# Turning the pooled keys of four batches on VectorE and moving them by DMA, in an attention and hidden-layer kernel

## The chip, the cores and the metric

The kernel runs on one core of a Trainium2 chip. The core has five engines with a queue of instructions each: TensorE (PE in the profile, with its weight loads as PEld) multiplies matrices and writes PSUM; VectorE (DVE), ScalarE (ACT) and GpSimd (POOL) work on elements; SyncE (SP) does no arithmetic here and issues DMAs. A DMA is carried out by 16 DMA engines that all queues share. Each engine takes its instructions in the order of the program and waits on semaphores for the others. SBUF is the memory of 128 partitions that the engines work in; PSUM, eight banks of 2 KB per partition, takes what TensorE writes.

The metric is the device time of one execution in microseconds. Less is better.

## The reference

The first half is attention over pooled keys and values, for 8 batches of 8 heads, 576 positions and 64 numbers per head, all f32:

```python
k_p = k.reshape(B, H, Sp, pool, D).mean(axis=3)      # Sp = 72 pooled keys, of 8 positions each
v_p = v.reshape(B, H, Sp, pool, D).mean(axis=3)
scores = scale * np.matmul(q, k_p.transpose(0, 1, 3, 2))
scores = scores - np.max(scores, axis=-1, keepdims=True)
attn = np.exp(scores)
attn = attn / (np.sum(attn, axis=-1, keepdims=True) + 1e-09)
x = np.matmul(attn, v_p)        # then (batch, position) become 4608 rows, the heads 512 columns
```

The second half takes these 4608 rows x 512 columns through two matrix products with a sine between them:

```python
h = x @ w_in                    # 512 -> 2048
s = np.sin(alpha * h)
g = h + s * s / (alpha + 1e-09)
out = g @ w_out                 # 2048 -> 512
```

## The kernel before, in words

**Stages.** After a head start (batch 0, some 20 us), the kernel runs nine units of about 55 us each, from 0 to 8. A unit computes the hidden values h and g of 512 rows of x (`hidden`, line 816), which it stores to DRAM; beside it runs the attention of a later batch. After the units, up to the end, the second product is computed (`outputs`, its matmuls at L1328). Both products use Strassen's scheme on 2 x 2 blocks, so that sums and differences of blocks are formed by VectorE and GpSimd, and TensorE does 7 block products in place of 8.

**Slots.** A unit has 28 slots: four groups J of 256 + 256 hidden columns, and seven block products (k = 0 to 6) in each. A slot's product is four matmuls of 256 columns (L844). `carry(u)` (line 1169) is a list written by hand: `at(slot, f)` puts a step into a slot, and in that slot its instructions are given to all engines, in between those of the products. So the order on each engine is fixed when the program is built, and no scheduler changes it.

**What a unit u of 1 to 6 carries.** It computes the attention of batch b = u + 1, whose rows are needed by the next unit. In the order of slots: the scores (`two_scores`, slots 3 and 5, matmuls at L317); the row maxima and differences on VectorE (`shifts`, L340 and L341); in slot 6 the load of the batch's values (`load_v`, L140 and L145); in slot 7 the load of the queries of batch u + 2 (`load_q`, L84 and L105); from slot 8 the exponentials on ScalarE, the normalization on GpSimd (L374), and the turn of the attention weights on VectorE in 32 x 32 blocks (`turn`, L501 to L511); in slot 14 sixteen DMAs which put the turned blocks into their places (`move`, L521, tile `aM`); in slots 23 and 24 the turn of the next queries (`turn_q`, L228 and L233), and their sixteen DMAs (L243); in slot 25 the products with the values (`all_values`, L610 and L623). The hidden values of each group J are stored by two DMAs (`store_g`, L1060) from one of two buffers `h`.

**The keys.** `load_k` (line 116) loads the keys of four heads by one DMA (L121) into a buffer `kvin`, of which there are two and which the values use too; two loads make a batch. GpSimd adds up the 8 positions of a pooled key in three additions per half (`pool_rows`, L131), and the sums come to the tile `kp`: 96 partitions, partition 24 hp + x for the head pair hp and the group x of three keys, and on each partition three keys j of two heads of 64 numbers. There is one buffer for `kp`. `k_t` (line 273) then turns them: three transposes on TensorE (L278), one for each j, into a bank of PSUM, from which one copy on VectorE (L279) brings them to `kblk`, with the three j woven together, so that the 72 keys of a head stand in a row. `kblk` has two buffers, for even and odd batches. The score matmuls have 64 queries as the stationary operand, read `kblk` as the moving one and write 72 columns of PSUM.

Before the change, unit u loads and adds up the keys of batch b + 1 in slot 12, and turns them in slot 26 of the same unit. They are read in slot 3 of the next.

**SyncE's queue.** Nearly all DMAs are issued by SyncE, in the order of the slots. The program gives them eight semaphores in turn, and lets each DMA wait for the one eight places before it.

Of the kernel before, what the change touches and what calls it, by code (L numbers as in the profile page):

```python
# [13 lines left out]
F32 = mybir.dt.float32  # L14
# [26 lines left out]
class Kernel:  # L41
# [216 lines left out]
    def attention(self, b):  # L258

        nc, D, H, Sp, NP, S = self.nc, self.D, self.H, self.Sp, self.NP, self.S  # L260
        kb, ex = self.kblk[b % 2], self.ex
# [11 lines left out]
        def k_t():  # L273
# [4 lines left out]
                nc.tensor.transpose(ps[:, j, :], kp[:, j].rearrange("p e d -> p (e d)"), self.ident[:NP * m, :NP * m])  # L278
            nc.vector.tensor_copy(out=kb[:].rearrange("p hp (x j) -> p j hp x", j=3), in_=ps.rearrange("p j (hp x) -> p j hp x", hp=NP))  # L279

        def q_t(i, copy=nc.scalar.copy):

            n = rows[i]
            x = self.qm[b][:n].rearrange("p (t hp x) -> p t hp x", t=5, hp=NP)[:, i]
            if b not in self.qt:
                self.qt[b] = self.qt_view(self.q_tile(0))
            ps = self.abank([P, NP, P])
            for hp in range(NP):
                nc.tensor.transpose(ps[:, hp, :n], x[:, hp], self.ident[:n, :n])  # L289
            copy(out=self.qt_tiles(b)[:, i, :, :n], in_=ps[:, :, :n])  # L290

        def columns(hp, i):

            if b < 2:
                if i == 4:
                    return [(0, self.qt_tiles(b)[:, 4, hp, 0:64])]
                return [(c, self.qt_tiles(b)[:, i, hp, c:c + 64]) for c in range(0, rows[i], 64)]
            if i < 4:
                at = self.q_at(i) + P * hp
                return [(64 * c, self.qt[b][:, at + 64 * c:at + 64 * c + 64]) for c in range(2)]  # L300
            return [(0, self.qt[b][:, 512 + 64 * hp:576 + 64 * hp])]

        def two_scores(j):

            x = (self.turn + 1) % 5
            tiles = []
            for i, banks in ((2 * j, (x, 7)), (2 * j + 1, (5, 6))):
                m = 6 if i == 3 else NP
                ps = [self.psum([P, m, Sp], c) for c in banks]
                tiles.append((i, m, ps))  # L310
                for t in (i, 4) if i == 3 else (i,):
                    for hp in range(NP):
                        r0, h = (64 * (hp // 2), NP + hp % 2) if t == 4 else (0, hp)
                        for r, q in columns(hp, t):
                            for e in range(2):
                                s = slice(64 * e, 64 * e + 64)
                                nc.tensor.matmul(ps[e][r0 + r:r0 + r + q.shape[-1], h, :], q[s], kb[s, hp, :], start=True, stop=True)  # L317
            for i, m, ps in tiles:
                self.shifts.append(lambda i=i, m=m, ps=ps: shifts(i, m, ps))
            two_shifts()  # L320
            if j == 0:
                two_shifts()

        def two_shifts():

            self.shifts.pop(0)()

        def shifts(i, m, ps):

            y = E(i).rearrange("p (e h) k -> p e h k", e=2)  # L330
            if i % 2:
                ps, y = [self.PS[:, 5:7, 0:m * Sp].rearrange("p e (h k) -> p e h k", h=m)], [y]
            else:
                y = y[:, 0], y[:, 1]
            for z, o in zip(ps, y):
                w = list(z.shape)[:-1]
                mx = self.sm.tile([P, 12], F32, name="mx2")[:, 0:m * (1 + i % 2)]
                if i % 2:
                    mx = mx.rearrange("p (e h) -> p e h", e=2)
                nc.vector.tensor_reduce(out=mx, in_=z, axis=AX, op=OP.max)  # L340
                nc.vector.tensor_tensor(out=o, in0=z, in1=mx.unsqueeze(len(w)).to_broadcast(w + [Sp]), op=OP.subtract)  # L341
# [258 lines left out]
        def all_values():  # L600
# [26 lines left out]
            for hp in hps:  # L627
                to_x(ps[hp].rearrange("p (t j) -> p j t", t=4), hp, 0, 512)
            to_x(rest, slice(0, 4), 512, 64)

        return SimpleNamespace(**{f.__name__: f for f in (k_t, q_t, products, score, two_scores, two_shifts, exp, norm, new_a, turn, move, values, values_rest, all_values,
                                                          k_head, k_last, q_head, rest_q, products_head, soft_shift, soft_exp, norm_head, norm_rest, a_head, a_rest)})


# [534 lines left out]
    def carry(self, u):  # L1169

        nc = self.nc
        x = defaultdict(list)
        at = lambda slot, f, *a: x[slot].append(lambda: f(*a))
        last = self.B - 1
        b = u + 1
        if u == 0:
            A0, A = self.att[:2]
            at(1, A0.rest_q)
            at(1, A0.a_head, 1, (5, 6, 2))
            at(1, self.refine)  # L1180
            at(2, A0.values, (2, 3), (2, 1), 1, 1)
            at(2, A0.score, 4)
            at(2, self.sums_of_x, 0, 2)
            at(2, self.sums_of_x, 0, 3)
            at(2, self.load_w_in_part, 2)
            at(2, self.load_w_in_part, 3)
            at(2, self.pairs_q, 1, (0, 1))
            at(3, self.pairs_q, 1, (2, 3, 4))
            at(4, self.combine_w_in, 1, (0, 1, 2, 3), self.nc.gpsimd)
            at(4, A.q_t, 0, self.nc.vector.tensor_copy)  # L1190
            at(4, A.q_t, 1, self.nc.vector.tensor_copy)
            at(4, A.k_t)
            at(7, self.load_v, 1)
            at(7, lambda: self.pool_v())
            for i in range(2):
                at((6, 11)[i], A.two_scores, i)
            at(13, A.two_shifts)
            for i in range(2, 5):
                at((8, 8, 9)[i - 2], A.q_t, i)
            at(9, A0.exp, 4)  # L1200
            for i in range(4):
                at((9, 9, 15, 15)[i], A.exp, i)
                at((10, 10, 16, 16)[i], A.norm, i)
                at((13, 13, 19, 19)[i], A.turn, i)
            at(8, self.combine_w_in, 2, (0, 1, 2, 3), self.nc.gpsimd)
            at(13, A0.norm_rest)
            at(17, self.combine_w_in, 3, (0, 1), self.nc.gpsimd)
            at(17, self.combine_w_in, 3, (2, 3), self.nc.gpsimd)
            at(22, A0.a_rest)
            at(24, lambda: A0.values_rest((5, 6, 7, (self.turn + 1) % 5)))  # L1210
            for r in (32, 96):
                at(3, self.nc.gpsimd.memset, self.aM[r:r + 32, :, 704:736], 0.0)
            at(19, A.move, range(3))
            at(20, A.move, (3,), nc.scalar, (0,))
            at(21, A.move, (3,), nc.scalar, (1,))
            at(26, A.all_values)
            at(9, self.load_q, 2)
            at(23, self.inner_w_in)
            for e in range(2):
                at(12, self.load_k, 2, e)  # L1220
                at(17, lambda e=e: self.pool_k[e]())
            at(27, self.att[2].k_t)
            turn = 23
        else:
            at(0, self.sums_of_x, u, 2)
            at(0, self.sums_of_x, u, 3)
        if 0 < u < last:
            A = self.att[b]
            for i in range(2):
                at((3, 5)[i], A.two_scores, i)  # L1230
            at(6, A.two_shifts)
            for i in range(4):
                at((8, 9, 10, 10)[i], A.exp, i)
                at((9, 10, 11, 12)[i], A.norm, i)
                at((12, 13, 13, 13)[i], A.turn, i)
            at(14, A.move, range(4))
            at(6, self.load_v, b)
            at(12, lambda: self.pool_v())
            for i in range(2):
                if b < last:  # L1240
                    at(12, self.load_k, b + 1, i)
                    at(12, lambda i=i: self.pool_k[i]())
            at(25, A.all_values)
            if b < last:
                at(26, self.att[b + 1].k_t)
            if 2 < u + 2 <= last:
                at(7, self.load_q, u + 2)
            at(2, self.inner_x, u)
            turn = 22
        elif u:  # L1250
            turn = None
        if turn and u + 2 <= last:
            for part in range(4):
                at(((turn, turn + 1) if u == 0 else (23, 24))[part] if part < 2 else turn + part, self.turn_q, u + 2, part)
        if u + 1 < self.NU:
            at(27, self.sums_of_x, u + 1, 0)
            at(27, self.sums_of_x, u + 1, 1)
        return x
# [336 lines left out]
```

## Time and profile before

| | us |
|---|---|
| median of three runs | 904.47 (903.34 to 905.92) |
| the profiled execution | 904.95 |
| its span, from the first to the last instruction | 903.2 |
| TensorE busy in it | 895.0 |
| VectorE, ScalarE, GpSimd busy | 681.0, 449.1, 212.6 |
| matmuls of the first product (L844), busy | 440.9 |
| score matmuls with `kblk` (L317), busy | 19.9 |
| transposes of the keys (L278), busy | 2.9 |
| the copies behind them (L279), busy | 3.9 |

A line of the chain of waits or of a timeline begins with a start and a length in us, then names the engine, the line of the program, what is done to which tiles, and how many instructions are merged; in square brackets stands how long the engine was idle before, and what ended that. An f32 matmul shows as two records (two passes), and a few records are missing from the trace. A transpose on TensorE shows as one. The granted clock of TensorE is 1.00 throughout. The units' products lie between 20 and 516 us of the span, and the scores of units 3 to 6 begin at 202.5, 257.8, 312.8 and 367.9.

### The profile page before, as it was taken

The numbers are of one execution on the slowest core, as the hardware profiler recorded it, in microseconds if no ns is written. First come the engines' busy times: TensorE is split into PE (matmuls) and PEld (weight loads), VectorE is DVE, ScalarE is ACT, GpSimd is POOL, SyncE is SP. The second block draws the span as 40 slices with busy tenths as digits, with TensorE's granted clock in tenths as the row PEclk, the third lists the DMA queues.
The fourth block names the chain that finished last, engine by engine and source line by source line (L and its number), as shares of the span: only waits on it lengthen the run. The fifth ranks groups of instructions, "written<-read, shape, count | busy, mean of one in ns | idle before, by whom it ended". The sixth has DMA issues, their size and how long they took to land.

```text
span 903.2 us, 17920 instructions
## 1 busy us (share of the span) xinstructions
PE 895.0 (99%) x7002; PEld 815.1 (90%) x7002; DVE 681.0 (75%) x1012; ACT 449.1 (50%) x1072; POOL 212.6 (24%) x216
## 2 busy tenths in 40 slices
PE   8999999999999999999999999999999999999998
PEld 5787888888888888888888999999999999999998
DVE  7685766768577685764557799979798888889895
ACT  5686776877768778687976611111111111111111
POOL 5688552824438253430000000000000000000000
PEclk9999999999999999999999999999999999999999
DMA  9965867759577595648217246261618162533401
GB/s 253 255 200 151 219 166 196 194 149 270 145 212 186 174 238 138 180 141 298 93 67 232 98 139 205 53 198 40 224 27 227 37 192 72 171 92 123 141 14 40
DMA packets 128746, 141.12 MB, mean 156 GB/s; under 512 B 46920, under 2 KB 95704, under 8 KB 128664
## 3 DMA queue, kind: packets, MB, share of 16 engines
q1 hardware_dynamic: 125880, 137.88, 53.5%
q10 hardware_dynamic: 2784, 2.11, 0.9%
q8 instruction: 55, 0.90, 0.4%
q14 instruction: 27, 0.22, 0.1%
HBM read 75.37 MB, written 47.19 MB: 136 GB/s over the span
## 4 chain that ended last, share of the span: by engine, by line
PE 95%; DVE 2%; ACT 2%; DMA 1%; POOL 0%; SPq 0%; ACTq 0%; issue 0%; DVEq 0%
PE PS L844 44%; PE PS L1328 41%; PE PS L1024 3%; PE PS L317 2%; PE PS L610 2%; PE PS L623 1%; DMA home<-in_k_dram 1%; DVE x L1283 1%; ACT s L1001 0%; DVE s L1283 0%; DVE r L1283 0%; ACT s L994 0%; PE PS L568 0%; PE PS L289 0%; PE PS L278 0%; PE PS L566 0%
## 5 line engine op out<-in xcount | busy, mean ns | idle before, releaser
L844 PE MATMUL PS<-home,a 128*128 128x256 f32 x1104 | 258.0, 381 | 0.4 <-DVE h L819 0.2
L844 PEld LDWEIGHTS PS<-home,a 128*128 128x128 f32 x1104 | 205.2, 190 | 33.3 <-issue 5.0
L844 PE MATMUL PS<-home,as 128*128 128x256 f32 x768 | 182.9, 382 | 0.5 <-ACT PS L820 0.5
L844 PEld LDWEIGHTS PS<-home,as 128*128 128x128 f32 x768 | 141.6, 190 | 20.6 <-ACT PS L820 1.2
L1378 POOL TENSOR_TENSOR cc<-cc,cb 128x576 f32<-128x576 f32 x1 | 2.0, 1980 | 501.8 <-DVE cb L1283 501.8
L1328 PE MATMUL PS<-s,wb 128*128 128x144 f32 x896 | 119.1, 286 | 0.0
L1328 PEld LDWEIGHTS PS<-s,wb 128*128 128x128 f32 x896 | 113.7, 190 | 0.1
L1001 ACT ACTIVATE s<-s,c 128x256 f32<-128x256 f32 (+1 forms) x228 | 113.5, 564 | 0.0
L819 DVE TENSOR_TENSOR h<-PS,p 128x512 f32<-128x512 f32 x72 | 49.2, 683 | 62.0 <-PE PS L844 36.9
L131 POOL TENSOR_TENSOR kvin<-kvin 96x768 f32<-96x768 f32 (+3 forms) x42 | 72.7, 1731 | 71.7 <-DMA kvin<-in_v_dram 69.3
L1456 ACT COPY PS<-PS 128x144 f32<-128x144 f32 x56 | 14.7, 263 | 144.8 <-PE PS L1328 138.1
L994 ACT ACTIVATE s<-h,al 128x256 f32<-128x256 f32 x144 | 65.6, 509 | 38.3 <-DVE h L819 38.1
L1328 PE MATMUL PS<-r,wb 128*128 128x144 f32 x512 | 73.3, 286 | 0.3 <-DVE r L1283 0.3
L1328 PE MATMUL PS<-s,a 128*128 128x144 f32 x512 | 73.2, 286 | 0.0
L994 ACT ACTIVATE s<-PS,al 128x256 f32<-128x256 f32 x144 | 60.2, 470 | 20.2 <-PE PS L844 19.2
L1046 DVE TENSOR_TENSOR h<-PS,s 128x512 f32<-128x512 f32 x36 | 24.7, 685 | 58.6 <-ACT s L1001 58.6
L1328 PEld LDWEIGHTS PS<-r,wb 128*128 128x128 f32 x512 | 67.1, 190 | 0.5 <-DVE r L1283 0.5
L1328 PEld LDWEIGHTS PS<-s,a 128*128 128x128 f32 x512 | 67.0, 190 | 0.0
L820 ACT COPY PS<-PS 128x512 f32<-128x512 f32 x72 | 41.5, 576 | 34.9 <-PE PS L844 30.1
L1476 ACT COPY PS<-PS 128x144 f32<-128x144 f32 x56 | 14.7, 263 | 88.1 <-PE PS L1328 88.1
L1046 DVE TENSOR_TENSOR h<-h,s 128x1024 f32<-128x1024 f32 x36 | 57.1, 1586 | 0.9 <-ACT s L1001 0.9
L1328 PE MATMUL PS<-x,wb 128*128 128x144 f32 x384 | 54.9, 286 | 0.0
(216 smaller groups left out, 1409.6 us busy)
## 6 DMA issues: line engine op xcount, KB each, us to landing
g_bridge<-h SPq DMA_DIRECT2D x72, 512.0 KB
r<-g_bridge SPq DMA_DIRECT2D x31, 1152.0 KB
out_dram<-o SPq DMA_DIRECT2D x122, 72.0 KB
kvin<-in_k_dram SPq DMA_DIRECT2D x14, 576.0 KB
q<-in_q_dram SPq DMA_DIRECT2D x7, 1024.0 KB
kvin<-in_v_dram SPq DMA_DIRECT2D x14, 512.0 KB
aM<-tr SPq DMA_DIRECT2D x54, 92.0 KB
aM<-tr SPq DMA_DIRECT2D x54, 88.0 KB
```

Source lines behind the costliest of these rows:

```text
L131: self.nc.gpsimd.tensor_tensor(out=t[..., 0:w] if w > D else out, in0=t[..., 0:w], in1=t[..., w:2 * w], op=OP.add)
L317: nc.tensor.matmul(ps[e][r0 + r:r0 + r + q.shape[-1], h, :], q[s], kb[s, hp, :], start=True, stop=True)
L610: nc.tensor.matmul(o[r:r + 64], w, x, start=start and i < 2, stop=False, skip_group_check=True)
L819: add = lambda o, x, y: nc.vector.tensor_tensor(out=o, in0=x, in1=y, op=OP.add)
L820: copy = lambda o, x: nc.scalar.copy(out=o, in_=x)
L844: nc.tensor.matmul(ps[:, jj, :], self.A[p][:, kk, f * P:(f + 1) * P], x[:, kk, :], start=(start and n == 0), stop=(kk == 1), skip_group_ch ...
L994: self.nc.scalar.activation(out=G.s[:, i, jj, j, :], in_=src[:, jj], func=AF.Sin, scale=self.al[:, f:f + 1])
L1001: self.nc.scalar.activation(out=x, in_=x, func=AF.Square, scale=self.c[:, f:f + 1])
L1024: nc.tensor.matmul(o, W[m][:, G.J - J0], X[m], start=start and n == 0, stop=True, skip_group_check=True)
L1046: add = lambda o, x, y: self.nc.vector.tensor_tensor(out=o, in0=x, in1=y, op=OP.add)
L1328: nc.tensor.matmul(out, W[:, J // 2, J % 2, :], A[:, J, :], start=(start and J == 0), stop=(J == self.NJ - 1), skip_group_check=True)
L1456: nc.scalar.copy(out=x1[:, 0, :], in_=x0[:, 1, :])
```

## The change

For batches 4 to 7 (the fifth to the eighth) `k_t` is replaced by two steps, and the scores read another layout.

- `k_turn`: one VectorE instruction transposes `kp` in 32 x 32 blocks, 96 partitions x 384 numbers, into a new tile `k_tr`. It is given in slot 7.
- `k_move`: twelve DMAs on SyncE's queue bring its blocks to `kblk`, each from 32 partitions to 32 partitions, three runs of 32 numbers (128 bytes) on each. They are given in slot 8, which on SyncE is behind the load of the queries in slot 7. In `kblk` the three j now stand apart, 96 numbers each.
- `keys`: the score matmuls of these batches read three runs of 24 numbers, and write each run to every third word of the PSUM row. The rows in PSUM come out as before, and nothing behind them changes.
- The loads: from unit 2 on, unit u loads the keys of batch b + 2 in slot 12, in place of b + 1, since they are turned in slot 7 of the next unit. Unit 1 loads batch 3 in slot 12 and turns it by `k_t` in slot 26 as before, and loads batch 4 as well: DMAs in slot 22, additions in slot 27. Unit 5 loads no keys any more.

On TensorE, four groups of three transposes are gone (at the end of units 2 to 5), and the 72 score matmuls of units 3 to 6 have other access patterns. On VectorE, four copies of slot 26 are gone and four transposes stand ahead of the additions of L1046 in slot 9. GpSimd has as many instructions as before, one batch's six of them a unit earlier each. SyncE has 48 DMAs more. ScalarE's queue is unchanged.

```diff
+        def k_turn():
+
+            kp = self.kp.pop(b)
+            self.k_tr = self.ap.tile([self.NP * (Sp // 3), 4 * Sp + 4 * Sp // 3], F32, name="k_tr")[:]
+            nc.vector.transpose(out=self.k_tr.rearrange("p (c j i) -> p j c i", c=4, j=3),
+                                in_=kp[:].rearrange("p j e d -> p j (e d)").rearrange("p j (c i) -> p j c i", i=32))
+
+        def k_move():
+
+            n = NP * Sp // 3
+            to = kb[:].rearrange("p h x -> p (h x)").rearrange("p (j n) -> p j n", j=3)
+            for c in range(4):
+                for a in range(3):
+                    nc.sync.dma_start(out=to[32 * c:32 * c + 32, :, 32 * a:32 * a + 32],
+                                      in_=self.k_tr[32 * a:32 * a + 32, n * c:n * c + n].rearrange("p (j i) -> p j i", j=3))
+
+        def keys(hp, s, out):
+
+            if b < 4:
+                return out, kb[s, hp, :]
+            m = Sp // 3
+            k = kb[s].rearrange("p h x -> p (h x)").rearrange("p (j n) -> p j n", j=3)
+            return out.rearrange("p (x j) -> p j x", j=3), k[:, :, m * hp:m * hp + m]
...
-                                nc.tensor.matmul(ps[e][r0 + r:r0 + r + q.shape[-1], h, :], q[s], kb[s, hp, :], start=True, stop=True)
+                                out, k = keys(hp, s, ps[e][r0 + r:r0 + r + q.shape[-1], h, :])
+                                nc.tensor.matmul(out, q[s], k, start=True, stop=True)
...
             for i in range(2):
-                if b < last:
-                    at(12, self.load_k, b + 1, i)
+                ahead = b + 1 + (u > 1)
+                if ahead <= last:
+                    at(12, self.load_k, ahead, i)
                     at(12, lambda i=i: self.pool_k[i]())
+                if u == 1:
+                    at(22, self.load_k, b + 2, i)
+                    at(27, lambda i=i: self.pool_k[i]())
             at(25, A.all_values)
-            if b < last:
+            if u == 1:
                 at(26, self.att[b + 1].k_t)
+            elif b < last:
+                at(7, self.att[b + 1].k_turn)
+                at(8, self.att[b + 1].k_move)
```

More of the change, by code (lines that the diff above doesn't have):

```diff
@@ L629, in all_values @@
             to_x(rest, slice(0, 4), 512, 64)
-        return SimpleNamespace(**{f.__name__: f for f in (k_t, q_t, products, score, two_scores, two_shifts, exp, norm, new_a, turn, move, values, values_rest, all_values,
+        return SimpleNamespace(**{f.__name__: f for f in (k_t, k_turn, k_move, q_t, products, score, two_scores, two_shifts, exp, norm, new_a, turn, move, values, values_rest, all_values,
                                                           k_head, k_last, q_head, rest_q, products_head, soft_shift, soft_exp, norm_head, norm_rest, a_head, a_rest)})
```

## The prediction

> **What bounds the kernel now.** I read the engines' line and the chain on the page first, then the chain piece by piece inside one unit, because the change touches only the units in which attention runs beside the first matrix product.
>
> ```profile
> PE 895.0 (99%) x7002; PEld 815.1 (90%) x7002; DVE 681.0 (75%) x1012; ACT 449.1 (50%) x1072; POOL 212.6 (24%) x216
> PE 95%; DVE 2%; ACT 2%; DMA 1%; POOL 0%; SPq 0%; ACTq 0%; issue 0%; DVEq 0%
> ```
>
> TensorE is busy for 99% of the span and carries 95% of the chain. What is taken from TensorE's own stream comes off the end one for one; what moves on another engine counts only if it makes TensorE wait. The chain over units 3 and 4 (start, length, what, how many) shows the two groups that the change edits, the transposes of the keys (L278) and the scores (L317):
>
> ```profile
> 193.62 0.25 PE PS L278 x3
> 193.86 8.66 PE PS L844 x40
> 202.53 1.31 PE PS L317 x62
> 203.83 3.65 PE PS L844 x16
> 207.49 1.46 PE PS L317 x76
> ...
> 243.34 2.33 PE PS L610 x43
> ...
> 248.68 0.44 PE PS L278 x3
> ...
> 303.93 0.25 PE PS L278 x3
> 358.99 0.25 PE PS L278 x3
> ```
>
> L844 gives the array's pace: 8.66 us for 40 records of 256 columns, 217 ns each, 0.85 ns a column. L610 is where TensorE first reads the moved attention weights, so 243.34 is the deadline for unit 3's moves. The timeline of SyncE's queue in the same unit (start, length, DMAs) shows what the key moves have to fit between:
>
> ```profile
> 207.49 2.68 SPq L145 DMA_DIRECT2D vr<-in_v_dram  x4
> 210.28 0.39 SPq L84 DMA_DIRECT2D q<-in_q_dram  x1
> 210.71 2.80 SPq L105 DMA_DIRECT2D q<-in_q_dram  x2
> 218.88 0.90 SPq L1060 DMA_DIRECT2D g_bridge<-h  x2
> 219.88 2.07 SPq L121 DMA_DIRECT2D kvin<-in_k_dram  x2
> 228.13 11.18 SPq L521 DMA_DIRECT2D aM<-tr  x16
> ```
>
> Two gaps are free, 213.5 to 218.9 and 222.0 to 228.1. The moves themselves are paced by issue, 11.18 / 16 = 0.70 us each. VectorE around the spot where it will turn the keys, and where it next needs those moves done:
>
> ```profile
> 213.20 1.06 DVE L341 TENSOR_TENSOR ex<-PS,mx 128x864 f32<-128x864 f32 x1
> 216.21 0.69 DVE L1046 TENSOR_TENSOR h<-PS,s 128x512 f32<-128x512 f32 x1 [1.96 <-ACT s L1001]
> ...
> 240.96 1.25 DVE L228 STREAM_TRANSPOSE tr<-q 128x1024 f32<-128x1024 f32 x1 [0.18 <-DMA aM<-tr]
> ```
>
> VectorE stands idle for 1.96 us at 214.26, and at 240.96 it has just waited for the last move, which so landed about 1.6 us after its issue ended at 239.31. TensorE's deadline is 2.4 us later.
>
> **Removed from TensorE.** Three transposes in each of units 2 to 5, for batches five to eight (one to eight are numbered from 0 in the code, so b = 4 to 7). Their pieces of the chain are 0.25, 0.44, 0.25 and 0.25 us: 1.19 us off the path. Nothing stood behind them: TensorE does not wait for the keys at L278 in these units, so no stall goes with them. By the Trainium skill, "TensorE: Matmul & The Clock Gate", Part 4, a transpose costs about 275 ns in a kernel; 12 of them would be an estimated 3.3 us and the sum would be 901.2 us. This trace has them at 243/246/273 ns from start to end, but three overlap with their neighbours and take 0.25 us of the chain, so I go by the chain.
>
> **Removed from and added to VectorE.** The copy L279 (540/548/566 ns) goes from between two additions of slot 26; TensorE's chain does not pass through it, so this is 0. Added is one block transpose of 96x384 per batch. Between the rows of 128x256 (401 ns) and 128x512 (688 ns) that is 0.54 us. It stands behind the last L341 of the scores and ahead of L1046, so it runs from 214.26 to 214.80, inside the idle 1.96 us: 0. Without that idle time, 0.54 us on VectorE four times, 2.2 us at most, and only if TensorE waited for it.
>
> **Changed on TensorE: the score matmuls of four batches.** 72 matmuls in two passes are 144 records a batch, 1.31 + 1.46 = 2.77 us on the chain. They now read the 72 keys as 3 runs of 24 and write column x of run j to word 3x + j of the PSUM row, so neighbours in time land 12 bytes apart. Reading in short runs is shown by L610: its 64-column matmuls read two runs of 32 words, and in the timeline four of them begin every 0.12 us (190.10, 190.22) in two quarters of the array, 60 ns a pair against 64 x 0.85 = 54 of streaming: free, or nearly. Writing PSUM at a stride is shown nowhere in the trace. Bounds: at best nothing (I exclude a gain, the columns being the same number). At worst each write takes two slots: 72 columns at 0.85 ns are 61 ns a record, four quarters of the array work at once, so 15.2 ns of the 18.3 ns that a record takes (1.46 us over 80) are streaming; doubled, that adds 15.2 x 144 = 2.2 us a batch, 8.8 us for four. The nearest rows: VectorE writing SBUF at this same 12-byte stride, L279, takes 548 ns for 288 elements, against 450 ns for an addition of 288 from PSUM written in a row (L341, 458 ns; 450 at L1283); ScalarE reading PSUM at a 512-byte stride, L537, takes 434 ns for 256, against 372 for a plain copy of 256 at L1028. So strides cost other engines a sixth to a fifth on engine paces of about one element per ns, and an f32 pass on TensorE, 0.85 ns a column, is no quicker than those. Most of such a fraction would sit in the 3.1 ns per record that are not streaming. I take 0 and keep 8.8 us as the upper end.
>
> The Trainium skill speaks against this edit: "SBUF — State Buffer", Door 1, and "PSUM — Partial Sum Buffer", Specifications (TRN2), say that PSUM has lines of 8 bytes, two f32 words, and that "any non-contiguous PSUM access pattern significantly slows down matmuls". No run so far shows a matmul that writes so; it is the first rival below.
>
> **Added to SyncE's queue.** 12 DMAs of 32 partitions x 3 runs of 128 bytes a batch, behind the load of queries and ahead of the store L1060, the load of keys L121 and the moves L521. Issue: the nearest rows are 0.67 us each (L145, 2.68 / 4), 0.70 (L521), and 1.40 (L105, 2.80 / 2, 32 partitions with four runs each, waiting included): 8.0 to 16.8 us, I take 0.67, since L105's pair waits. Bytes on the rings: 147 KB in 1152 pieces; the page's 128746 packets at 54.9% of 16 engines' 903 us are 62 ns a packet, so at most 1152 / 16 x 62 ns = 4.5 us, at the 220 GB/s of these stretches 0.7 us. Taken: 1 us.
> Walk through unit 3: the first move issues at 214.8, when the turned keys are there. The program gives SyncE's DMAs eight semaphores in turn, each DMA waiting for the eighth before it; the sixth key move therefore waits for the load of queries. In two-microsecond windows the DMA share is 1.05, 1.07, 1.10 and 0.95 up to 218, then 0.43 in 218 to 220: the load lands at about 220.5. Seven more issues end at 225.2; the store (0.90) and the keys' load (2.07), with their gaps, end at 228.3, against 228.13 where L521 starts today. The store and load land some 5 us later than now, behind which the first moves queue: the last move lands 0.2 to 1.2 us later, and 2.4 us are free. Cost 0, cover 1.2 us or more.
> Who else waits: the hidden values' buffer stored at L1060 is written again only at 234.49 (VectorE, L819). GpSimd's sums of the keys start at 228.16 and end at 236.1; 5 us later is still ahead of its next work at 253.41. The turned keys are read a whole unit later, at 257.8. VectorE's L228 may start a microsecond late and has 3.15 us idle before 248.77.
>
> **Moved: the loads of keys, one unit sooner.** Unit 1 loads two batches. The second load enters SyncE's queue at 130.5, between a store and the moves of queries at 134.65, and lands near 137; GpSimd's six extra additions (1.88 + 1.31 + 0.68 us, twice) run 137 to 145 in an idle stretch of 16.96 us that ends at 143.0. The sums of x behind them come 2 us late and are first read at 168.5 (L1024). Cost 0; unit 5 loads no keys at all, which frees 2.07 us there.
>
> **Sum.** -1.2 + 0 + 0 + 0 = -1.2 us. The profiled execution took 904.95 us (span 903.2 and 1.8 around it), the median of the runs 904.47 (903.34 to 905.92). From the median: 903.3 us, a change of 0.13%, inside the 0.3% that a measurement of this kernel can tell from none.
>
> **Rivals.**
> 1. *Strided PSUM writes slow the scores* (slower). One mechanism, in L317's 576 records of four batches. At two slots a write, +8.8 - 1.2: 912.1 us. It crosses 0.3% at +3.9 us, a slowing of the streaming by 1.44. For: no row shows such a write, and the skill's sentence is about just this. [...] Chance 0.30.
> 2. *The key moves make the attention moves late* (slower). It decides when seven issues behind the query load take over 1.0 us each instead of 0.67, or that load lands over 2 us later. At 1.40 us an issue, L521 starts 5.3 us late, TensorE waits 2.9 us at L610 in units 2 to 4 and 0.8 in unit 5: 9.5 - 1.2, 912.8 us. For: the queue is on the edge at 228. Against: L145, L521 and L243 (10.61 us for 16) all issue at 0.66 to 0.70. Chance 0.08, most of it at some 907.
> 3. *The transposes cost more than their pieces* (faster). If nothing of them overlapped, each would cost its whole 246 ns: 12 x 0.246 = 2.95 us, 901.5 us. For: one piece of four is 0.44. Against: three are 0.25, a third of that. Chance 0.06.
> 4. The change does nothing: it removes 12 named instructions, so only as the forecast's sum, which I can't tell from none anyway.
>
> **How the numbers follow.** Forecast 0.52, rivals 0.30, 0.08, 0.06, other ways to lose 0.04. Within 0.3%: the forecast less 0.03 of scatter, and 0.03 for a mild rival 1: 0.52. Slower by over 0.3%: 0.27 + 0.08 + 0.04 = 0.39. Faster by over 0.3%: rival 3 and the scatter, 0.09. The range goes from rival 3 to rival 1's end, 901.5 to 912.2; the forecast's own is 901.8 to 905.0.
>
> **What would show it.** Right: no transpose of keys after unit 1 in the chain, L610 to L610 distances of 54.8 in place of 55.1 us, the scores' two pieces still 1.31 and 1.46 us in units 3 to 6. Wrong: pieces above 1.6 and 1.8 us, with records above 20 ns (rival 1); idle TensorE before L610, or L521 starting after 230 in unit 3's place (rival 2).

## The result, and the profile after

| | before | after |
|---|---|---|
| median of five runs, us | 905.43 (903.34 to 905.92) | 916.86 (913.24 to 919.95) |
| profiled execution, us | 904.95 | 913.24 |
| its span, us | 903.2 | 911.4 |

The changed kernel is slower: the ratio is 1.0125, 95% interval 1.0107 to 1.0143. The forecast was 903.3 us, no change. The time is 4.7 us above the end of the range; slower by over 0.3% had a chance of 0.39, mostly by another rival than the one that came.

TensorE's busy time hardly moved, but its share of the chain did. The lines for the engines and for the chain on the page of the changed kernel:

```profile
PE 897.5 (98%) x6990; PEld 814.4 (89%) x6990; DVE 674.9 (74%) x1012; ACT 448.6 (49%) x1072; POOL 208.5 (23%) x216
PE 79%; DMA 8%; DVE 4%; SPq 4%; ACT 3%; issue 1%; POOL 1%; ACTq 0%; DVEq 0%; POOLq 0%
```

Twelve matmul records are gone, as the change says, and the chain, 95% TensorE before, is now 79% TensorE, 8% DMA and 4% SyncE's queue. So nothing got slower on TensorE itself: it waits.

To see where, take the distance in time from the last value products (L623 before, L648 after) of one unit to those of the next, in the profiled executions:

| up to unit | 2 | 3 | 4 | 5 | 6 |
|---|---|---|---|---|---|
| before, us | 55.16 | 55.06 | 55.26 | 55.06 | 55.06 |
| after, us | 58.36 | 57.68 | 57.61 | 54.78 | 54.79 |

Units 5 and 6 are 0.28 us shorter, close to the forecast's pieces of 0.25 us. Units 2, 3 and 4 are 3.20, 2.62 and 2.35 us longer. Together that is +7.6 us; another 0.6 us arose ahead of unit 1, which the change does not touch: the last value products of unit 0 begin at 81.87 before and 82.48 after, and at 81.4 to 83.8 in the other executions profiled here. That makes the 8.2 us between the spans. The table already narrows the cause: unit 5 moves keys as units 2 to 4 do, but it loads none, and it loses nothing.

The chain of waits of the changed kernel in unit 3 (start, length, what, how many) no longer runs through TensorE's products alone but through loads:

```profile
213.57 11.64 DMA q<-in_q_dram
...
231.81 8.37 DMA kvin<-in_k_dram
...
245.66 2.10 DMA aM<-tr
...
247.85 1.25 DVE tr L228
249.09 0.59 DVE h L1071
...
249.72 2.40 PE PS L635 x39
```

Read it backwards from the value products at 249.72. They wait for VectorE's sum L1071, which frees a PSUM bank; that stands behind the turn of the queries, L228; that waits for the last attention move (`aM<-tr`); that is late since the moves of L546 were held by the load of keys; and that load was late since it stands on SyncE's queue behind the key moves, whose sixth waits for the load of queries. The timeline of SyncE's queue in unit 3 of the changed kernel, to be compared with the same stretch before:

```profile
213.57 0.39 SPq L84 DMA_DIRECT2D q<-in_q_dram  x1
214.00 2.09 SPq L105 DMA_DIRECT2D q<-in_q_dram  x2
218.30 11.35 SPq L294 DMA_DIRECT2D kblk<-k_tr  x12
229.75 1.05 SPq L1085 DMA_DIRECT2D g_bridge<-h  x2
230.90 2.04 SPq L121 DMA_DIRECT2D kvin<-in_k_dram  x2
233.03 13.22 SPq L546 DMA_DIRECT2D aM<-tr  x16
```

Unit 3 runs 3.82 us later by then (the last products of unit 2 begin at 194.37, against 190.55). Less that, the sixteen moves start at 229.21, 1.1 us later than before, and their issue ends at 242.43, against 239.31: 3.1 us later. They take 13.22 us where they took 11.18. In unit 2 it is 13.84 us where it was 11.13. The waits of SyncE's queue name what held it (total us, times, longest):

```profile
SPq L294 <- DMA q<-in_q_dram: 11.5, 4, 3.0
SPq L546 <- DMA kvin<-in_k_dram: 9.2, 6, 2.8
```

The second line is most of the loss: six waits of the attention moves for loads of keys, 3.1 us a unit, in three units. In unit 3 the seventh move is issued at 237.67 and the eighth at 240.20, where the others mostly follow each other every 0.63 us. Eight places before the seventh and eighth of the sixteen moves stand the two loads of keys. That was so before as well, but then the loads were issued at 219.88 and had landed when the seventh move's turn came, some 4 us into the sixteen.

The last part is VectorE. Its timeline around the wait in unit 2, and TensorE's (in brackets the idle time before, and what ended it):

```profile
190.17 1.25 DVE L228 STREAM_TRANSPOSE tr<-q 128x1024 f32<-128x1024 f32 x1 [3.93 <-DMA aM<-tr]
191.34 0.65 DVE L1071 TENSOR_TENSOR h<-PS,s 128x512 f32<-128x512 f32 x1
```

```profile
190.19 1.08 PE L635 MATMUL PS<-aM,vm 64*64 64x512 f32 x4 [1.39 <-DMA aM<-tr]
192.04 0.33 PE L635 MATMUL PS<-aM,vm 64*64 64x64 f32 x4 [0.78 <-DVE h L1071]
```

TensorE stops twice: for the moves, and then for L1071, which VectorE could give only behind the 1.25 us of L228. Before the change neither stop existed, as the moves had landed in time.

The rival that had the most weight, strided writes to PSUM, is not there. The pieces of the scores in unit 5, with the new layout:

```profile
321.36 1.30 PE PS L342 x62
326.31 1.46 PE PS L342 x76
```

They were 1.31 and 1.46 us.

### The profile page after: what moved, and what is told of

It is laid out like the page before. It is cut to its first block, busy times and chain, and to the rows that moved or that the text cites. A ratio compares the mean times of both kernels' runs of the same rounds, so it can differ in the third digit from the quotient of the medians.

```text
span 911.4 us, 17936 instructions
## 1 busy us (share of the span) xinstructions
PE 897.5 (98%) x6990; PEld 814.4 (89%) x6990; DVE 674.9 (74%) x1012; ACT 448.6 (49%) x1072; POOL 208.5 (23%) x216
## 4 chain that ended last, share of the span: by engine, by line
PE 79%; DMA 8%; DVE 4%; SPq 4%; ACT 3%; issue 1%; POOL 1%; ACTq 0%; DVEq 0%; POOLq 0%
PE PS L1360 40%; PE PS L869 31%; DMA q<-in_q_dram 3%; DMA kvin<-in_k_dram 3%; PE PS L635 2%; SPq L546 2%; PE PS L1049 2%; ACT s L1026 1%; PE PS L342 1%; DVE h L1071 1%; PE PS L648 1%; DMA aM<-tr 1%; DMA kvin<-in_v_dram 1%; DVE s L1315 1%; SPq L294 1%
## 5 line engine op out<-in xcount | busy, mean ns | idle before, releaser
L844 DVE TENSOR_TENSOR h<-PS,p 128x512 f32<-128x512 f32 x72 | 49.2, 683 | 66.6 <-PE PS L869 41.7
L131 POOL TENSOR_TENSOR kvin<-kvin 96x768 f32<-96x768 f32 (+3 forms) x42 | 70.3, 1674 | 99.4 <-DMA kvin<-in_v_dram 70.5
L1071 DVE TENSOR_TENSOR h<-PS,s 128x512 f32<-128x512 f32 x36 | 24.6, 684 | 56.3 <-ACT s L1026 56.3
L1360 PE MATMUL PS<-s,we 128*128 128x144 f32 x384 | 54.9, 286 | 0.0
```

Source lines behind the costliest of these rows:

```text
L131: self.nc.gpsimd.tensor_tensor(out=t[..., 0:w] if w > D else out, in0=t[..., 0:w], in1=t[..., w:2 * w], op=OP.add)
L844: add = lambda o, x, y: nc.vector.tensor_tensor(out=o, in0=x, in1=y, op=OP.add)
L1071: add = lambda o, x, y: self.nc.vector.tensor_tensor(out=o, in0=x, in1=y, op=OP.add)
L1360: nc.tensor.matmul(out, W[:, J // 2, J % 2, :], A[:, J, :], start=(start and J == 0), stop=(J == self.NJ - 1), skip_group_check=True)
```

## The experiments

The theory after this reading: everything that the change does to TensorE is as forecast; the loss comes from what twelve more issues do to SyncE's queue, by way of its semaphores taken in turn. The rivals: something of the new layout or of the earlier loads costs after all, or the small packets of the key moves slow the other DMAs.

**One part away: no key moves.** (Line numbers of the changed kernel hold, unless lines are put in.)

```diff
-                at(8, self.att[b + 1].k_move)
```

> Leaves out the twelve key moves of batches 4 to 7, so their scores read the keys of two batches earlier; the turn on VectorE, the sooner loads and the strided score matmuls stay. Theory (the moves, through SyncE's queue, make the attention moves late): the loss is gone and only the gain of the removed transposes is left, 905.4 - 1.2 = 904.2 us, TensorE waits nowhere before the value products. Rival (the sooner loads or the score layout cost the time): 913 us or more, as in the changed kernel.

Measured: 904.34 us (902.03 to 905.16), ratio to the kernel before 0.9982 (0.9972 to 0.9991). The distances are 55.07, 54.78, 54.78, 54.79 and 54.78. Turns, layout, strided PSUM writes and earlier loads are all still in it, so these together cost nothing, and the whole loss comes with the moves.

**One part alone: loads one unit sooner, turned on TensorE as before.**

```diff
-            if b < 4:
+            if True:
...
-                at(7, self.att[b + 1].k_turn)
-                at(8, self.att[b + 1].k_move)
+                at(8, self.att[b + 1].k_t)
```

> The loads one unit sooner alone: batches 4 to 7 are turned by TensorE and copied by VectorE as before, in slot 8 of the next unit, with the old layout and no key moves. Theory: no change, 904.5 to 906.5 us. Rival (the loads collide with something where they now stand): 909 us or more, with TensorE idle in units 1 to 4.

Measured: 905.41 us (903.94 to 906.59), ratio 0.9995 (0.9986 to 1.0004). Loading sooner costs nothing and brings nothing.

**Key loads behind the attention moves.**

```diff
-                    at(12, self.load_k, ahead, i)
-                    at(12, lambda i=i: self.pool_k[i]())
+                    at(15 if u > 1 else 12, self.load_k, ahead, i)
+                    at(15 if u > 1 else 12, lambda i=i: self.pool_k[i]())
```

> The changed kernel with the loads of keys of units 2 to 4 put behind the attention moves (slot 15 in place of 12), all else the same. Theory (the loads of keys, late behind the key moves, hold up the attention moves through the semaphore that the seventh and eighth share with them, and fill the rings ahead): sixteen attention moves take 10 to 11.2 us again, no wait of TensorE, 904.2 us. Rival (the issue of twelve more DMAs and the wait for the load of queries are enough by themselves): attention moves still end 3 us late, 910 us or more.

Measured: 905.67 us (903.69 to 907.12), ratio 0.9999 (0.9990 to 1.0007). The same 48 key moves are made in the same places; only two loads of keys a unit stand behind the attention moves instead of ahead. SyncE's timeline of this kernel in unit 3:

```profile
214.76 11.05 SPq L294 DMA_DIRECT2D kblk<-k_tr  x12
225.91 1.04 SPq L1085 DMA_DIRECT2D g_bridge<-h  x2
227.82 10.92 SPq L546 DMA_DIRECT2D aM<-tr  x16
238.84 0.99 SPq L121 DMA_DIRECT2D kvin<-in_k_dram  x2
```

The sixteen are back at 10.92 us, with the twelve just ahead of them. So it is not the number of issues or of packets, but the loads that got in between. Up to unit 5 this kernel still has one long distance, 55.73 us. Its waits on VectorE tell why:

```profile
DVE h L844 <- DMA g_bridge<-h: 8.1, 2, 4.6
```

The second store of the hidden values now stands behind the loads of keys, lands late, and holds the buffer that L844 writes.

**TensorE's pause filled, in the wrong bank.** Twelve matmuls on constants ahead of the value products of units 2 to 4; they add no result.

```diff
+    def keep_busy(self):
+        for _ in range(12):
+            self.nc.tensor.matmul(self.psum([P, 4, P], (self.turn + 1) % 5), self.full[:], self.full[:].unsqueeze(1).to_broadcast([P, 4, P]), start=True, stop=True)
...
+            if 1 < u < 5:
+                at(25, self.keep_busy)
```

> The changed kernel with twelve matmuls on constants ahead of the value products of units 2 to 4, where TensorE idles for 3.4 us, nothing else changed. Theory (the runs of 915 to 920 us are those in which the clock was lowered after such a pause): every run at a granted clock of 1.000 and 912.5 to 914.5 us. Rival (the scatter comes from the waits themselves): runs still between 913 and 920 us.

Measured: 925.05 us (923.24 to 926.83), ratio 1.0212 (1.0195 to 1.0230). Missed: the bank is the one that L1071 frees, so the added matmuls waited for it too, filled no pause, and came on top. (In the changed kernel's profile the idle time that the expectation puts at 3.4 us is 1.39 and 0.78 us in unit 2, with products between them.) But the profile of this run shows what that of the changed kernel doesn't, the clock. Windows of two microseconds around the pause in unit 3 (window, length, busy us of each engine with instructions, granted clock, DMA share, GB/s):

```profile
248.00:250.00 2.00, 1.04 (x7) 0.81 (x6) 0.86 (x1) 2.00 (x5) 0.00 (x0) 1.00 0.85 288
250.00:252.00 2.00, 0.99 (x4) 0.43 (x4) 2.00 (x3) 0.15 (x1) 0.00 (x0) 0.91 0.75 282
252.00:254.00 2.00, 2.00 (x6) 0.76 (x5) 1.80 (x3) 0.00 (x0) 0.00 (x0) 0.50 0.07 17
254.00:256.00 2.00, 2.00 (x26) 0.93 (x28) 0.00 (x0) 0.00 (x0) 0.00 (x0) 0.73 0.58 139
```

TensorE is idle for 1.97 us up to 251.01. From about 251.6 to 255.1 the granted clock is half: (0.18 + 1.00 + 0.54) us of clock missing is 1.7 us, and a half over 3.4 us. Behind the pause of unit 4, 2.73 us, it is the same; behind that of unit 2, 2.94 us, the clock stays at 1.00.

**The key moves parted, loads behind.** Three of the twelve moves at their place, nine behind the store; the loads as in the late-load run.

```diff
+                    if (3 * c + a < 3) != (part == 0):
+                        continue
...
-                at(8, self.att[b + 1].k_move)
+                at(8, self.att[b + 1].k_move, 0)
+                at(13, self.att[b + 1].k_move, 1)
```

> Of the twelve key moves of a unit the first three are issued where all twelve were, the other nine behind the store of g (list entry 13), and the keys of units two to four are loaded behind the attention moves (entry 15). Everything is computed. Theory (the moves cost by what they hold up on SyncE's queue: with three of them ahead, the store's semaphore, eight places back, is one that came free before the load of queries; with the key loads behind, no attention move waits for a long load): store issued at the times of before (163.6 and 218.9), the sixteen L546 within 11.2 us and starting by 173.3 and 228.4, VectorE's wait for g_bridge of the late-load run gone; the kernel without key moves, 904.3: 903.8 to 904.9. Rival (the nine later moves make the attention moves late): L546 starts after 229.5 in unit 3 and the run is over 907.

Measured: 904.57 us (903.85 to 907.22), ratio 0.9990 (0.9982 to 0.9998). The first store is back in time, and the sixteen take 10.74 and 10.75 us in units 2 and 3, 11.33 in unit 4. Of the expectation one part failed: up to unit 5 the distance is 56.06 us, so the wait for `g_bridge` stayed. As the first store is early here, it must be the second one that causes it, behind the loads of keys.

**VectorE's order.**

```diff
         if part == 0:
+            self.finish_before()
             for e in range(2):
...
                 nc.vector.transpose(out=out, in_=x)
-                if e == 0:
-                    self.finish_before()
```

> The changed kernel, with VectorE's first sum of last_h, L1071, which frees the PSUM bank of the value products, ahead of the two transposes of queries that wait for the attention moves, instead of between them. Theory (of the loss of some 2.8 us in each of units 2 to 4, the moves' lateness is about 1.5 and VectorE's order the rest, as its 1.25 + 0.6 us stand between the landed moves and the bank): value products start when the moves land, at about 190.2, and run on without the second stop at 192.04 (0.78 us) and the drain before it; gain 1.0 to 1.4 us in each of the three units; run 908.5 to 910.5 at full clock. Rival (the order is nothing, something else stands at 192): 912.5 or more at full clock.

Measured: 909.87, 909.95, 913.96 and 914.50 us, median 911.96, ratio 1.0062 (1.0043 to 1.0081). Two executions had a granted clock of 1.000 on the mean, and these are the first two times; the other two had 0.996. At full clock that is 3.3 us less than the changed kernel's 913.24, 1.1 us a unit, as expected: about a third of the 9.0 us by which its units 2 to 4 exceed those of the kernel without key moves. The second stop is gone from TensorE's timeline. The profiled execution, one of those at 0.996, shows the pause of unit 2, now one piece, and the clock behind it:

```profile
192.15 1.12 PE L634 MATMUL PS<-aM,vm 64*64 64x512 f32 x6 [2.33 <-issue]
```

```profile
190.00:192.00 2.00, 0.00 (x0) 0.00 (x0) 0.00 (x0) 0.94 (x2) 0.00 (x0) 1.00 0.69 200
192.00:194.00 2.00, 1.85 (x24) 1.52 (x28) 1.87 (x2) 0.00 (x0) 0.00 (x0) 0.52 1.01 377
194.00:196.00 2.00, 2.00 (x30) 1.32 (x22) 2.00 (x3) 0.90 (x3) 0.00 (x0) 0.62 0.16 52
```

**TensorE's pause filled, in the bank that is free.** As above with six matmuls, and `(self.turn + 4) % 5`.

> The changed kernel with six matmuls of 128x512 (bf16, on constants, result unused) ahead of the value products in units 2 to 4, in the PSUM bank that ScalarE's copy to p5 frees (about 189.3), so that they lie in TensorE's pause (188.8 to 192). They add no result. Theory (the scatter of the changed kernel, 913.2 to 920.0, is the clock: in the run with twelve such matmuls in the wrong bank the profile shows 0.50 of full clock for about 3.4 us behind the pauses of units 3 and 4): no pause is over 2 us long, granted clock at least 0.999 in all runs, time 912.5 to 914.5. Rival (the scatter is not from the pauses): mean clocks of 0.992 to 0.997 again, and times of 915 to 920.

Measured: 915.14, 916.10, 916.20 and 914.20 us, ratio 1.0108 (1.0095 to 1.0121). The mean clock is 0.999 or 1.000 in all four, and they lie within 2.0 us instead of 6.7. The clock part of the theory held. The level is 1.1 us above the expected end. In the profile the three distances are 58.83, 58.11 and 59.12 us, 2.4 us more than without the fill, mostly in unit 4. That the fill costs this is not shown: the attention moves are issued later too, by 0.4 us in unit 2 already, which is ahead of the first fill.

**The key moves on GpSimd's queue.**

```diff
-                    nc.sync.dma_start(out=to[32 * c:32 * c + 32, :, 32 * a:32 * a + 32],
+                    nc.gpsimd.dma_start(out=to[32 * c:32 * c + 32, :, 32 * a:32 * a + 32],
```

> The changed kernel with the twelve key moves of a unit issued from GpSimd's queue instead of SyncE's. The same bytes and packets move between the same places. Theory (the loss is from SyncE's queue and the order in the rings, not from the moves' 576 packets): L121 (key loads) and L546 back at the times of before (164.6 and 173.3 in unit 2; 219.9 and 228.1 in unit 3), first value products at 188.1 and 243.3; run 904 to 906.5, the upper end for GpSimd, which may start pooling the values later. Rival (the small packets themselves slow the loads down): L546 late by 3 us as in the changed kernel, 911 or more.

Measured: 941.04 us (939.34 to 945.12), ratio 1.0397 (1.0377 to 1.0418). Missed, by another wait. The key loads are indeed back in time, at 164.16 in unit 2. But GpSimd issues in order too. Its timeline in unit 2:

```profile
163.67 4.50 POOL L294 DMA_DIRECT2D kblk<-k_tr  x8
...
172.63 0.55 POOL L294 DMA_DIRECT2D kblk<-k_tr  x1 [0.30 <-DMA kblk<-k_tr]
173.19 5.09 POOL L399 TENSOR_TENSOR ex<-ex,sm 128x576 f32<-128x576 f32 x4
```

The normalization L399, begun at 165.89 in the changed kernel, waits behind the moves until 173.19, so the weights are turned late and the attention moves begin at 180.53. This run says nothing against the theory, and little for it: only that the sixteen take 10.69 us again once the loads of keys are early. (The 576 packets of the expectation are a slip: twelve moves have 32 x 3 runs each, 1152 a unit, and the page of the changed kernel counts 5376 more packets under 512 bytes, 1344 for each of four units.)

**Loads behind the second store too.** The parted moves, with the loads of keys in slot 20 instead of 15 ("list entry" below is the slot).

> As the run with the key moves parted three and nine, but the keys of units two to four are loaded at list entry 20, behind the second store of g as well. Everything is computed. Theory (what that run still lost was the second store standing behind the two key loads, so that VectorE waited for g_bridge in unit 5: 56.06 us from last value product to last value product there, against 54.79 without): every distance between the last value products of units 2 to 6 within 54.7 to 55.1, no wait of VectorE for g_bridge over 1 us; 902.5 to 904.2, faster than the kernel before by 0.1 to 0.3%. Rival (the loads now hold up the moves of queries, which are issued behind them at entries 25 and 26, and through them the scores): 905 or more.

Measured: 904.14 us (902.45 to 905.42), ratio 0.9985 (0.9976 to 0.9994). The distances are 55.07, 54.78, 54.79, 54.78 and 54.78, those of the kernel without key moves, and VectorE waits for no store. This version keeps all of the change and is 0.15% faster than the kernel before. Its chain in unit 3 is TensorE's alone again (numbers of lines are two higher), and SyncE's timeline has room:

```profile
242.26 0.44 PE PS L1051 x4
242.71 2.33 PE PS L637 x43
245.03 1.09 PE PS L650 x8
```

```profile
214.68 2.00 SPq L296 DMA_DIRECT2D kblk<-k_tr  x3
218.22 0.91 SPq L1087 DMA_DIRECT2D g_bridge<-h  x2
221.38 5.80 SPq L296 DMA_DIRECT2D kblk<-k_tr  x9
227.48 10.91 SPq L548 DMA_DIRECT2D aM<-tr  x16
238.49 1.07 SPq L1087 DMA_DIRECT2D g_bridge<-h  x2
239.65 2.06 SPq L121 DMA_DIRECT2D kvin<-in_k_dram  x2
```

**Fewer moves ahead of the loads, more behind.** The changed kernel, with five key moves at their place and seven in slot 13, behind store and loads; the loads stay in slot 12. This is the run that tells the semaphores from the crowd: if the semaphores are the cause, moving issues out of the way must not help much.

> The changed kernel with the first five key moves of a unit at their place and the other seven at list entry 13, behind the store and the two key loads. Everything is computed. Theory (SyncE holds a DMA until the one eight places before it on the queue has landed): the store waits for the first load of queries, eight places before it, so the key loads are issued some 2 us later than before and not 8; but of the seven moves the fifth waits for the store, the seventh for the first key load, and the first L546 for the second key load, so that L546 starts only when the key loads have landed: about 177 in unit 2 and 231 to 234 in unit 3, its sixteen then in 11 us. Units 2 to 4 lose 3 to 5 us each against before: 911 to 918. Rival (what delays the moves is the data in the rings, or the eleven microseconds of twelve issues ahead of the loads; then five issues instead of twelve ahead of them take most of the loss away): L546 within 2 us of the times of before (173.3 and 228.1) and 904 to 908.

Measured: 911.29 us (908.85 to 912.02), ratio 1.0055 (1.0039 to 1.0071). SyncE's timeline in unit 2, and two lines of what its queue waited for:

```profile
167.33 0.90 SPq L1087 DMA_DIRECT2D g_bridge<-h  x2
168.33 2.06 SPq L121 DMA_DIRECT2D kvin<-in_k_dram  x2
170.44 4.68 SPq L296 DMA_DIRECT2D kblk<-k_tr  x7
177.03 10.32 SPq L548 DMA_DIRECT2D aM<-tr  x16
```

```profile
SPq L548 <- DMA kvin<-in_k_dram: 4.6, 3, 1.8
SPq L296 <- DMA kvin<-in_k_dram: 1.9, 3, 1.3
```

This execution runs 1.0 us behind that of the changed kernel by the end of unit 1. Less that, the loads of keys are issued 5.1 us earlier, and yet the attention moves start 1.4 us later: the first of them now waits for a load of keys eight places ahead (once in each of the three units, by the first line of waits). Then they run through in 10.32 us. Less its lag behind the kernel before, the start is 175.4 in unit 2 (177 was expected) and 231.1 in unit 3 (231 to 234). The time is at the low end of the 911 to 918 expected, and outside the rival's 904 to 908. But the loss of a unit was expected too high: the distances are 56.43, 57.38 and 57.04 us, 1.27, 2.32 and 1.78 more than before, not 3 to 5, and 1.6 us of the profiled time arose ahead of unit 1. So two thirds of the changed kernel's loss in these units stay, and one third goes.

## Why the prediction was wrong

**What bounds the kernel: right.** TensorE sets the end, and only what makes it wait costs.

**Removed transposes, 1.19 us: right, and a little low.** In the kernel without key moves the four distances that lose a group of three, up to units 3 to 6, are 0.28, 0.48, 0.28 and 0.28 us shorter than before, 1.32 us together.

**VectorE's copy and turn, 0: right.** The turn takes 0.56 us against 0.54, in the idle time where it was put, and the kernel without key moves loses nothing by it.

**Strided PSUM writes, 0 taken and 8.8 us kept as the upper end: the choice was right, and rival 1, with its chance of 0.30, did not come.** The score matmuls have the same 222, 223 and 274 ns (least, median, most) in both kernels, though 576 of the 1008 records now write words 12 bytes apart. The sentence of the Trainium skill, "SBUF — State Buffer", Door 1, that any non-contiguous PSUM access slows matmuls, does not hold for these: f32, 72 columns, in three interleaved runs. Why they are free is not shown. The prediction's reason does not carry it: by its own rows of 401 and 688 ns VectorE needs 1.12 ns an element, so an f32 pass, at 0.85 ns a column, is quicker than that and not "no quicker".

**Loads one unit sooner, 0: right** (0.9995 when done alone).

**SyncE's queue, "the last move lands 0.2 to 1.2 us later", cost 0: this step failed.** Its walk was right up to the start of L546: 1.1 us later in unit 3 where it said 0.2, with seven issues in the time that it gave them. It went wrong behind that. It used the rule that a DMA waits for the one eight places before it on the key moves (the sixth waits for the load of queries), but not on the sixteen attention moves themselves. It said that the loads of keys would land some 5 us later, and let the moves only "queue behind" their data; it did not ask which moves wait for them by semaphore. The seventh and eighth do, and stood still for 3.1 us a unit. The last move was issued 3.4 us later in unit 2 and 3.1 us later in unit 3; of the 3.1, the later start is 1.1 and the longer run of the sixteen 2.0. The parted runs bear this out: with the loads behind, no loss; with fewer issues ahead but the loads still within eight places, two thirds of it. No run changed the number of semaphores, so what the moves would lose behind the loads' data alone stays open.

**"2.4 us are free": wrong as well.** The step took TensorE's first reading of the moves, 243.34, as their deadline. But in between stands VectorE's order. In the trace of before:

```profile
240.96 1.25 DVE L228 STREAM_TRANSPOSE tr<-q 128x1024 f32<-128x1024 f32 x1 [0.18 <-DMA aM<-tr]
242.12 0.65 DVE L1046 TENSOR_TENSOR h<-PS,s 128x512 f32<-128x512 f32 x1
```

```profile
243.27 0.65 PE L610 MATMUL PS<-aM,vm 64*64 64x512 f32 x6
```

L228 starts as soon as the last move is there, and behind it L1046, from 242.12 to 242.77, frees the bank that the matmuls of 64 columns write. Their first is merged into the line of L610 and begins at 243.28. So the last move had 0.5 us in unit 3, not 2.4, and 3.1 us of lateness less 0.5 is the 2.6 us by which this unit grew. In unit 2 there was nothing to spare: L1046 ended at 188.16 there, and L610 had begun at 188.10. The forecast's own 0.2 to 1.2 us would already have cost something. The step saw that L228 may start late and found idle time behind it; it did not ask what L228 holds up. With that sum taken out of the way, 3.3 us came back.

**Rival 2: the right place, the wrong condition, and a chance that left out a second way.** It was to decide when issues take over 1.0 us each (they took 0.64) or the load of queries lands 2 us later (0.9, from 220.5 to 225.21 less 3.82). Neither happened, and TensorE waited at the value products all the same, in units 2 to 4 as it said. Of its signs, idle TensorE before the value products came; L546 starting after 230 did not (229.2). The rival was priced by the start of L546 alone; that the sixteen moves could be stopped after they had started was a second way to the same wait, and its chance of 0.08 left that out.

**What no step had: the clock.** The medians lie 11.4 us apart, the spans of the profiled executions, both at full clock, only 8.2. The five runs of the changed kernel had mean granted clocks of 1.000, 0.992, 0.993, 0.997 and 0.997 for 913.24, 919.95, 917.31, 915.68 and 916.86 us. Time multiplied by clock, an estimate of the time at full clock, is 913.2, 912.6, 910.9, 912.9 and 914.1 us: the clock explains about half of the scatter of 6.7 us, or more, as these clocks are rounded. That the lowered clock comes from the pauses is shown by the fill in the free bank, which took it away in all four runs.

## What to carry to other kernels

Where a queue gives its DMAs semaphores in turn, each DMA has a deadline for the one that many places behind it: to put short DMAs ahead of long loads is cheap only if, afterwards, no urgent DMA stands within the turn behind a load that has become late. Walk the whole queue with that rule, not only the DMAs that are added. Then take as the deadline of the urgent one not only its own reader, but whatever stands behind any waiting reader in that engine's order, and put long loads behind the urgent moves and stores, where their lateness meets nobody.

## What the runs showed of the hardware

- **A pause of some two microseconds can halve TensorE's clock.** After 1.97 and 2.73 us idle (fill in the wrong bank) and 2.33 us (VectorE's order) the granted clock was half for about 3.4 us; after 2.94 us, in the first of these runs, it stayed at 1.00. The Trainium skill, "TensorE: Matmul & The Clock Gate", Part 1, has a half clock that lasts for a window of about 3.4 us, and windows that run free of the kernel; the length agrees with these traces, and free windows would be a reason why one pause is hit and another is not, which no run here tests. It puts the fall after an idle window of about 3.4 us; here the longest single gaps were shorter.
- **An f32 matmul writes PSUM words at a stride of three as fast as in a row,** for 72 columns: 223 ns in the median in both kernels.
- **DMAs issued by GpSimd take its time:** eight took 4.50 us and single ones 0.55, in order with its arithmetic.
